# Bank choice, late evictions, a shared copy and earlier loads in a fused attention and Fourier-mixing kernel

## The chip, the cores and the metric

The kernel runs on one core of a Trainium2 chip. The metric is the device time of one execution in microseconds (us), the median of several runs. In the profile, PE is the matmul engine (PEld its weight loads), DVE the vector engine, ACT the scalar engine, POOL the GpSimd engine; SP only issues DMAs. L658 means line 658 of the kernel before.

## What is computed

Sequence length S = 2048, width D = 512, H = 32 heads of 16. All data are float32.

```python
g = sigmoid((x * gate_w).sum(-1, keepdims=True))
q, k, v = heads(x @ wqkv)
a = merge(softmax(q @ k.T * 16**-0.5) @ v) @ wo         # attention, 32 heads
b = Cr @ (x @ Wr.T) - Ci @ (x @ Wi.T)                   # real part of a 2-D DFT, dense matrices
out = g * a + (1 - g) * b
```

## The kernel before, in words

Heads go in 16 pairs, one head on each half of the PE's rows (j = 0 and 1, partitions 0 to 63 and 64 to 127). Two matmuls on different halves run beside each other, so the PE's work comes in slots of two.

Softmax needs the maximum of each query's scores before the exponentials, so each pair's scores are computed twice. A **scan** is a score matmul of 128 queries by 512 keys whose bank of PSUM is reduced to maxima by DVE (`scan`, L699 and L701). A **score** is the matmul for the exponentials (`score`, L668), read by ACT (L658), which writes a tile e in SBUF; there are 17 of these. Each step of 128 keys by 1024 queries has four scores (two of each half), and its **values** are four fp32 matmuls of e into one bank, `pvb` (`pv`, L678), each recorded as two. There are 512 steps, 32 for each pair; after every 16 the sums in `pvb` are copied to SBUF (`quotients`, L710) and later divided (`divide`). **Products** (`fill`, L919) are the matmuls of the large DFT, split in high and low parts, in banks z0 and z1. 48 products for each half make a group of 128 rows, and its two sums are evicted by DVE (`close` in `spectral`, L828 and L830) in the place where the last product is issued.

The program has four stages:

- **Front**: projections and the small DFT (`products`, L340 and L356), with the first 368 scans woven in, one pair of scans in 2.05 slots (`beside`, L186; ACT does a first pass, L190, and DVE a second, L192). `load_scan_beside` loads the keys and queries of the next head pair, 16 DMAs on ACT's queue, one every four slots, from the 37th scan of the first pair and the 21st of the others on. Their buffers are a ring of 12 (`piece`), in which the large weight loads (`load_w`, L408, on SP's queue) take turns too.
- **Single steps**: 42 rounds m of two steps, without products: `e0 e1 c0 c1 e0 e1` and then the values of one step. `values(2 * m + i)` gives the values of the step before the one just scored.
- **Fill rounds**: rounds 42 to 233, of two steps each: 8 scores, 6 scans and 16 products, then the values of two steps.
- **Mix rounds and end**: rounds 234 to 255, scores with the products of the output projection, and the last sums.

The order within a round is written out by hand. In a fill round it is

```python
"c0 e1 c0 e1 s0 s1 s0 s1 s0 s1 e0 s1 c0 e1 s1 s0 c1 e0 s1 s0 s1 s0 s0 c1 e1 s0 e0 s1 e0 c1"
```

where c is a scan, e a score, s a product, and the digit the half. We call the scans in their order S1 to S6 and the scores E1 to E8: the round runs S1 E1 S2 E2 E3 S3 E4 S4 E5 S5 E6 E7 E8 S6, with products between them. A group of products ends with the last `s0` and the last `s1` of a round, every sixth round, ahead of S6.

Scores and scans of a fill round share five banks, b0 to b4. Which bank one takes is settled by a planner, `Banks`, that keeps a clock of its own while the program is written: a bank is reckoned free 635 ns after the start of its exponential or 735 ns after that of its reduce. Of the five banks it takes the one with the least `max(s, free)`, plus 30 ns where the bank last served the other kind; among equals, the one longest free. In the single steps seven banks are in use: b0 to b3 for scores and b4, z0, z1 for scans.

Of the kernel before, what the change touches and what calls it, by code (L numbers as in the profile page):

```python
# [32 lines left out]
SCANS = 64  # L33
TOTAL = SCANS * NP
FRONT = 5 * SCANS + 48
# [6 lines left out]
SINGLES = 42  # L42
# [17 lines left out]
def build(tc, x, xT, wqkv, wo, wrT, wiT, cr, ci, gate, out):  # L60
    nc = tc.nc
    with ExitStack() as ctx:
# [55 lines left out]
        class Rows:  # L118

            def __init__(self):  # L120
                self.q, self.k = [None, None], [None, None]
# [129 lines left out]
        with ExitStack() as px:  # L251
# [11 lines left out]
            def after(n, f, *args):  # L263

                count[0] += 1
                due.append((slots[0] + n, count[0], f, args))

            def run_due(force=False):
                while True:
                    ready = [d for d in due if force or d[0] <= slots[0]]  # L270
                    if not ready:
                        return
                    d = min(ready, key=lambda d: d[:2])
                    due.remove(d)
                    d[2](*d[3])

            def load_scan_beside(p):
                rows, loads = scanned.setdefault(p, Rows()), []
                for part in PARTS:
                    load_part(rows, None, p, part, nc.scalar if p else nc.sync, kf_d, True, loads.append)  # L280
                for n, load in enumerate(loads):
                    after((4 if p else 2) * n, load)

            def scan_at(spacing):
                pace[0] = spacing
# [1 line left out]
            def beside():  # L287

                slots[0] += 1
                run_due()  # L290
                if pace[0] is None:
                    return
                pace[1] += 1.0 / pace[0]
                while seen[0] < FRONT and pace[1] >= 1.0:
                    pace[1] -= 1.0
                    n = seen[0]
                    if n % SCANS == (36 if n < SCANS else 20) and n - n % SCANS + SCANS < FRONT:
                        load_scan_beside(n // SCANS + 1)
                    if n == FRONT - SCANS + 8:
                        used[0] = Rows()  # L300
                        for part in PARTS:
                            load_part(used[0], "use", 0, part, nc.sync, k_d, True)
                    if n == FRONT - SCANS + 30:
                        first_rows.append(Rows())
                        for part in PARTS:
                            if part != "q0" or FRONT % SCANS < SCANS // 2:
                                load_part(first_rows[0], "scan", FRONT // SCANS, part, nc.sync, k_d, True)
                    scan_folded(n, 0, scan_bank)
                    done = behind(n - 1)
                    seen[0] += 1  # L310
                    if seen[0] == FRONT:
                        done = behind(n)
                    if done is not None and done % SCANS == SCANS - 1:
                        for d, part in enumerate(shift(done // SCANS)):
                            after(3 + 4 * d, part)

            def behind(n):
                if n in FOLDED:
                    scan_folded(n, 1, scan_bank)
                    return n  # L320

            behind_, ends = [], {}
# [61 lines left out]
            if True:  # L384
# [197 lines left out]
                while behind_:  # L582
                    follow()
                    beside()
# [5 lines left out]
        with ExitStack() as pa:  # L590
# [4 lines left out]
            def bank(tag, name="s"):  # L595
                return psl.tile([P, 512], F32, tag=tag, name=name)
# [3 lines left out]
            pvb = bank("pv", "pvb")  # L600
# [11 lines left out]
            class Banks:  # L612

                slot, late, gap, load, group, weights, second = 226.0, 425.0, 93.0, 207.0, 854.0, 103.0, 56.0
                switch = 30.0
                period, release = {"e": 475.0, "c": 682.0}, {"e": 635.0, "c": 735.0}
                names = [f"b{i}" for i in range(5)] + ["z0", "z1"]

                def __init__(self):
                    self.t, self.port, self.rows, self.swap = 0.0, 0.0, [0.0, 0.0], [0.0, 0.0]  # L620
                    self.free, self.last, self.count = [0.0] * 7, list("eeeeccc"), 7
                    self.engine, self.values = {"e": 0.0, "c": 0.0}, False

                def take(self, kind, j):
                    if self.values:
                        t = self.t = self.port = self.t + self.load - self.weights
                        self.rows, self.swap, self.values = [t, t], [t, t + self.second], False
                    s = max(self.port, self.swap[j])
                    if kind != "s":
                        group = (range(4) if kind == "e" else range(4, 7)) if self.count == 7 else range(5)  # L630
                        b = min(group, key=lambda b: (
                            max(s, self.free[b]) + self.switch * (self.last[b] != kind), self.free[b]))
                        self.last[b] = kind
                        s = max(s, self.free[b])
                    self.port = s + self.weights
                    self.t = self.swap[j] = max(self.port, self.rows[j], self.t + 6.0)
                    self.rows[j] = self.t + self.slot
                    if kind == "s":
                        return None
                    a = max(self.engine[kind], self.t + self.late)  # L640
                    self.engine[kind], self.free[b] = a + self.period[kind], a + self.release[kind]
                    return self.names[b]
# [64 lines left out]

            def quotients(p, h):
                ob = ap.tile([P, 512], F32, tag="ob", name="ob", bufs=2)
                nc.vector.tensor_copy(ob, pvb)  # L710
                lc = sm.tile([P, 16], F32, tag="lc", name="lc")
                for n, (c, j, r) in enumerate(quads):
                    nc.gpsimd.dma_start(lc[32 * n:32 * n + 32, :],  # L713
                                        ob[r + DH:r + VC, :].rearrange("p (s e) -> p s e", e=16))
                return p, h, ob, lc
# [200 lines left out]
            def emit(pr_, j, ps):  # L916
                group = pr_.group
                group.count[j] += 1
                nc.tensor.matmul(ps, pr_.lhs(j), pr_.rhs(j), start=group.count[j] == 1,  # L919
                                 stop=group.count[j] == group.size)  # L920
                if group.count[j] == group.size:
                    group.close(j, ps)

            def fill(j):

                if at[j] == len(stream):
                    stream.extend(next(source))
                pr_ = stream[at[j]]
                at[j] += 1
                banks.take("s", j)  # L930
                if pr_.enter and pr_.done == 0:
                    pr_.enter()
                if j not in pr_.group.banks:
                    pr_.group.banks[j] = bank(f"z{j}", "z")
                emit(pr_, j, pr_.group.banks[j])
                pr_.done += 1
                if pr_.leave and pr_.done == 2:
                    pr_.leave()

            freed = []  # L940
            staged, now = {}, [0]
            operands = output_operands()

# [76 lines left out]
            def values(n):  # L1020
                while valued[0] < n:
                    pv(valued[0])
                    valued[0] += 1

            for m in range(MACROS):
# [12 lines left out]
                p, half = divmod(m, NB)  # L1038
# [18 lines left out]
                n = min(scans)  # L1057
# [3 lines left out]
                if m < SINGLES:  # L1061
                    for i in range(2):
                        for k, token in enumerate(ORDERS[(count_ + 1 - i) // 2].split()):
                            {"e": score, "c": scan}[token[0]](int(token[1]))
                            if late and k == 3:
                                late.pop(0)()
                        values(2 * m + i)
                    continue
                for k, token in enumerate(ORDERS[count_, sizes[m]].split()):
                    {"e": score, "c": scan, "s": fill}[token[0]](int(token[1]))  # L1070
                    if late and k in (6, 13, 20):
                        late.pop(0)()
                values(2 * m)
            assert min(scans) == TOTAL, scans
            for step in (STEPS - 2, STEPS - 1):
# [15 lines left out]
            ob = ap.tile([P, 512], F32, tag="ob", name="ob", bufs=2)  # L1091
# [19 lines left out]
            c, ps = halves_[0], spread[0]  # L1111
# [8 lines left out]
            c, ps = halves_[1], spread[1]  # L1120
# [39 lines left out]
```

## Time and profile before

| | |
|---|---|
| runs before | 1748.30, 1748.83, 1749.85 us; median 1748.83 |
| profiled execution, its own time | 1747.27 us |
| its span in the profile | 1745.50 us |
| PE, ACT, DVE, POOL busy | 99%, 77%, 72%, 39% of the span |
| front | to about 351.7 us |
| single steps | to about 525 us |
| fill rounds | to about 1614 us |
| mix rounds and end | to 1745.5 us |

Times in rows are microseconds from the span's start. In a row of the timeline the first number is the start, the second the time to the end of the last of its instructions (x5 means five in a row); a bracket gives the idle time of that engine just before, and what ended it. A matmul's row that begins together with its weight load is about 0.11 us longer than the others: the load's time is in it.

### The profile page before, as it was taken

How to read it: one execution, taken by the hardware profiler on the slowest of the kernel's cores; microseconds unless marked ns; L12 is line 12 of the kernel's file. 1: busy time of each engine (PE TensorE's matmuls, PEld its weight loads, DVE VectorE, ACT ScalarE, POOL GpSimd, SP SyncE). 2: the span in 40 equal slices, each digit the busy share in tenths (PEclk: the TensorE clock that was granted, in tenths of full speed). 3: DMA queues.
4: the chain of work that ended last, by engine and by line, in shares of the span. 5: the costliest groups of instructions: out<-in, count | busy, mean ns of one | idle time of the engine just before them, and what ended most of it. 6: DMA issues, size and time to landing. Idle time of an engine off the chain costs nothing.

```text
span 1745.5 us, 36709 instructions
## 1 busy us (share of the span) xinstructions
PE 1721.8 (99%) x13657; PEld 1037.1 (59%) x13657; DVE 1264.3 (72%) x2385; ACT 1351.7 (77%) x2589; POOL 688.2 (39%) x860
## 2 busy tenths in 40 slices
PE   8999999999999999999999999999999999999998
PEld 7776788743445555555555555556555555555554
DVE  5598899866667777777777777777777777777433
ACT  5588988799997777777777777777777777777785
POOL 0263301353654443444444434434443443443121
PEclk9999999999999999999999999999999999999999
DMA  7575233564442333232333257323332422425522
GB/s 260 203 233 153 80 122 124 174 199 124 137 128 83 94 96 96 63 109 62 87 88 94 67 155 218 106 83 102 96 87 81 126 76 79 114 85 147 150 57 100
DMA packets 140003, 206.59 MB, mean 118 GB/s; under 512 B 58848, under 2 KB 61392, under 8 KB 139824
## 3 DMA queue, kind: packets, MB, share of 16 engines
q1 hardware_dynamic: 94992, 167.46, 31.4%
q0 software_dynamic: 41056, 27.86, 6.1%
q10 hardware_dynamic: 3776, 8.92, 1.8%
q8 instruction: 107, 1.75, 0.4%
q14 instruction: 72, 0.59, 0.1%
HBM read 137.89 MB, written 65.81 MB: 117 GB/s over the span
## 4 chain that ended last, share of the span: by engine, by line
PE 93%; DVE 1%; DMA 1%; issue 1%; ACT 1%; POOL 0%; SPq 0%; DVEq 0%; ACTq 0%
PE pvb L678 27%; PE z L919 23%; PE s L699 14%; PE s L668 14%; PE xy L340 6%; PE s L186 5%; PE xy L356 4%; DMA wraw<-wrT 0%; ACT fold L190 0%; DVE y L864 0%; DMA lc<-ob 0%; DVE fold L192 0%; DMA q_d<-el 0%; SPq L156 0%; DVE mx L701 0%
## 5 line engine op out<-in xcount | busy, mean ns | idle before, releaser
L658 ACT ACTIVATE e<-s 128x512 f32<-128x512 f32 x2048 | 1075.8, 600 | 298.9 <-PE s L668 251.2
L701 DVE TENSOR_REDUCE mx<-s 128x1 f32<-128x512 f32 x1312 | 860.3, 686 | 294.6 <-PE s L668 200.1
L668 PE MATMUL s<-qs,ks 50*128 50x512 f32 x2048 | 640.6, 425 | 0.0
L699 PE MATMUL s<-ks,qs 48*128 48x512 f32 x1312 | 500.9, 427 | 1.0 <-DVE mx L701 0.5
L678 PE MATMUL pvb<-e,va 128*17 128x512 f32 x4096 | 497.2, 595 | 0.0
L919 PE MATMUL z<-b,chi 64*128 64x512 f32 x2060 | 485.7, 392 | 0.0
L668 PEld LDWEIGHTS s<-qs,ks 50*128 50x128 f32 x2048 | 333.8, 184 | 118.3 <-ACT e L658 74.7
L699 PEld LDWEIGHTS s<-ks,qs 48*128 48x128 f32 x1312 | 215.4, 185 | 202.0 <-issue 118.2
L919 PE MATMUL z<-b,clo 64*128 64x512 f32 x1030 | 307.8, 392 | 0.0
L919 PEld LDWEIGHTS z<-b,chi 64*128 64x128 f32 x2060 | 280.7, 186 | 32.0 <-issue 0.8
L192 DVE CUSTOM_DVE_ANT_0 fold<-s,fold 128x512 f32<-128x512 f32 x368 | 242.8, 689 | 32.1 <-ACT fold L190 13.9
L186 PE MATMUL s<-ks,qs 48*128 48x512 f32 x736 | 237.4, 403 | 6.3 <-ACT fold L190 5.9
L244 POOL CAST chi<-craw 128x512 fp32r<-128x512 f32 x126 | 77.4, 614 | 399.1 <-PE z L919 390.3
L190 ACT ACTIVATE fold<-s 128x512 f32<-128x512 f32 x368 | 204.3, 604 | 34.2 <-PE s L186 28.3
L678 PEld LDWEIGHTS pvb<-e,va 128*17 128x17 f32 x4096 | 90.0, 96 | 218.9 <-issue 217.7
L919 PEld LDWEIGHTS z<-b,clo 64*128 64x128 f32 x1030 | 157.1, 186 | 17.0
L245 POOL TENSOR_TENSOR clo<-craw,chi 128x512 fp32r<-128x512 f32 x126 | 161.8, 1284 | 10.5
L186 PEld LDWEIGHTS s<-ks,qs 48*128 48x128 f32 x736 | 135.4, 185 | 45.0 <-ACT fold L190 17.8
L713 POOL DMA_DIRECT2D lc<-ob x124 | 63.2, 515 | 228.1 <-DVE ob L710 227.2
L356 PE MATMUL xy<-w,b 64*128 64x512 f32 x384 | 122.4, 403 | 0.0
L340 PE MATMUL xy<-w,b 64*128 64x512 f32 x384 | 118.1, 395 | 0.0
L864 DVE SCALAR_TENSOR_TENSOR y<-z,g,y 128x512 f32<-128x512 f32 x44 | 32.5, 749 | 65.3 <-PE z L919 63.6
(128 smaller groups left out, 1505.1 us busy)
## 6 DMA issues: line engine op xcount, KB each, us to landing
craw<-cr SPq DMA_DIRECT2D x64, 256.0 KB
craw<-ci SPq DMA_DIRECT2D x64, 256.0 KB
qs<-q_d SPq DMA_DIRECT2D x110, 128.0 KB
ks<-k_d SPq DMA_DIRECT2D x108, 128.0 KB
ab_d<-ab SPq DMA_DIRECT2D x32, 256.0 KB
y_d<-y SPq DMA_DIRECT2D x32, 256.0 KB
b<-bs_d SPq DMA_DIRECT2D x32, 256.0 KB
o_d<-oh POOLq DMA_DIRECT2D x28, 256.0 KB, 9.5
```

What stands on the lines that cost most here:

```text
L186: nc.tensor.matmul(ps, rows.q[qb // 8][b:b + 48, qb % 8 * P:(qb % 8 + 1) * P], rows.k[c // 2][b:b + 48, c % 2 * 512:(c % 2 + 1) * 512], st ...
L190: seen_by(nc.scalar.activation(fold[j], ps, AF.Relu))
L192: seen_by(nc.vector.tensor_tensor_reduce(out=fold[j], in0=ps, in1=fold[j], scale=1.0, scalar=-3.0e38, op0=ALU.add, op1=ALU.max, accum_out= ...
L245: sub(lo, raw, hi.bitcast(F32))
L340: ins = nc.tensor.matmul(ps, lhs[64:P], rhs[64:P], start=False, stop=last)
L356: nc.tensor.matmul(ps, lhs[0:64], rhs[0:64], start=n == 0, stop=False)
L658: nc.scalar.activation(e, ps, AF.Exp, scale=SCALE)
L668: nc.tensor.matmul(ps, rows.k[kb // 8][b:b + 50, kb % 8 * P:(kb % 8 + 1) * P], rows.q[h][b:b + 50, c * 512:c * 512 + 512], start=True, sto ...
L678: nc.tensor.matmul(pvb[r:r + VC, :], va[:, kb, 2 * p + j, :], es[step][c, j][0], start=kb == 0, stop=kb == NB - 1, tile_position=(0, r))
L699: nc.tensor.matmul(ps, rows.q[qb // 8][b:b + 48, qb % 8 * P:(qb % 8 + 1) * P], rows.k[c // 2][b:b + 48, c % 2 * 512:(c % 2 + 1) * 512], st ...
L701: nc.vector.tensor_reduce(mx[p][:, j, qb, c:c + 1], ps, axis=AX.X, op=ALU.max)
L919: nc.tensor.matmul(ps, pr_.lhs(j), pr_.rhs(j), start=group.count[j] == 1, stop=group.count[j] == group.size)
```

## The change

Six edits:

1. The DMAs of `load_scan_beside` for pairs after the first are three slots apart, not four.
2. They start with the 29th scan of the first pair, not the 37th, and with the 9th of the others, not the 21st.
3. `Banks` takes the bank with the earliest `free`, and the 30 ns for a change of kind are gone. In the single steps scores have five banks (b0 to b3 and z0), scans two (b4 and z1).
4. From round 42 on, `pvb` is copied by ACT (columns 0 to 255) and DVE (256 to 511), not by DVE alone.
5. The evictions of a group that ends in a round are issued behind all scans and scores of the round, ahead of its values.
6. In single steps the values are two steps behind the scores, not one.

```diff
-                    after((4 if p else 2) * n, load)
+                    after((3 if p else 2) * n, load)
...
-                    if n % SCANS == (36 if n < SCANS else 20) and n - n % SCANS + SCANS < FRONT:
+                    if n % SCANS == (28 if n < SCANS else 8) and n - n % SCANS + SCANS < FRONT:
                         load_scan_beside(n // SCANS + 1)
...
-                switch = 30.0
...
-                    self.free, self.last, self.count = [0.0] * 7, list("eeeeccc"), 7
+                    self.free, self.count = [0.0] * 7, 7
...
-                        group = (range(4) if kind == "e" else range(4, 7)) if self.count == 7 else range(5)
-                        b = min(group, key=lambda b: (
-                            max(s, self.free[b]) + self.switch * (self.last[b] != kind), self.free[b]))
-                        self.last[b] = kind
+                        group = ((0, 1, 2, 3, 5) if kind == "e" else (4, 6)) if self.count == 7 else range(5)
+                        b = min(group, key=lambda b: self.free[b])
...
-                nc.vector.tensor_copy(ob, pvb)
+                if now[0] < SINGLES:
+                    nc.vector.tensor_copy(ob, pvb)
+                else:
+                    nc.scalar.copy(ob[:, 0:256], pvb[:, 0:256])
+                    nc.vector.tensor_copy(ob[:, 256:512], pvb[:, 256:512])
...
                 if group.count[j] == group.size:
-                    group.close(j, ps)
+                    closing.append((group, j, ps))
...
-                        values(2 * m + i)
+                        values(2 * m + i - 1)
                     continue
...
+                for group, j, ps in closing:
+                    group.close(j, ps)
+                closing.clear()
                 values(2 * m)
```

More of the change, by code (lines that the diff above doesn't have):

```diff
@@ L932, in fill @@
                     pr_.enter()
+                assert not closing or pr_.group is closing[0][0], "a group ends within a round"
                 if j not in pr_.group.banks:
@@ L938, in fill @@
                     pr_.leave()
-            freed = []
+            freed, closing = [], []
             staged, now = {}, [0]
```

## The prediction

> **What bounds the kernel now.** I read the busy time by stage first, then the chain of work that ended last, then the timeline of single rounds. The profiled execution took 1747.27 us, its span is 1745.50.
>
> ```profile
> span 1745.5 us, 36709 instructions
> 0.00:351.70 351.70, 337.77 (x2696) 265.72 (x2696) 279.61 (x832) 273.37 (x536) 103.39 (x101) 0.99 0.52 168
> 351.70:525.00 173.30, 173.14 (x1193) 69.72 (x1193) 116.36 (x190) 172.84 (x342) 92.88 (x132) 1.00 0.51 149
> 525.00:1614.00 1089.00, 1088.49 (x8780) 634.96 (x8780) 816.82 (x1287) 810.78 (x1529) 465.56 (x592) 1.00 0.35 99
> 1614.00:1745.50 131.50, 122.44 (x997) 66.69 (x996) 51.52 (x79) 94.70 (x185) 26.40 (x37) 0.99 0.36 103
> ```
>
> The columns behind the length are the busy times of PE, PEld, DVE, ACT and POOL, then clock, DMA share and GB/s. PE seems full everywhere, but its ends are modelled, so its busy share can't show a short wait. In the single steps (second row) ACT is full too, and the timeline of ACT shows it without any gap:
>
> ```profile
> 351.70 173.28 ACT L658 ACTIVATE e<-s 128x512 f32<-128x512 f32 x341
> ```
>
> 341 exponentials in 173.28 us are 0.508 us each. **The single steps are ACT's**, and no order of banks or values there can bring anything. In the fill rounds ACT and DVE are busy three quarters of the time, and the chain of waits lies on PE. It gives the rounds' lengths, by the starts of the values' matmuls:
>
> ```profile
> 530.40 1.84 PE pvb L678 x16
> 536.05 1.84 PE pvb L678 x16
> 541.71 1.84 PE pvb L678 x16
> 547.36 1.84 PE pvb L678 x16
> 553.02 1.84 PE pvb L678 x16
> 558.86 1.84 PE pvb L678 x16
> 564.65 1.84 PE pvb L678 x16
> ...
> 1609.18 1.89 PE pvb L678 x16
> ```
>
> A plain round takes 5.65 us (541.71 to 547.36). The one from 553.02 takes 5.84: a group of products ended just before it. The one from 558.86 takes 5.79: `pvb` is copied in it. From the first to the last row lie 189 rounds in 1078.78 us, 10.9 more than 189 times 5.65. Counted from the code, 31 of them follow the end of a group and 23 hold a copy: 31 x 0.19 + 23 x 0.14 = 9.1 of the 10.9.
>
> **Plain rounds (edit 3).** Where a plain round loses time shows in its timeline (weight loads first, then reduces and exponentials):
>
> ```profile
> 546.16 0.39 PE L919 MATMUL z<-b,clo 64*128 64x512 f32 x1
> 546.17 0.18 PEld L699 LDWEIGHTS s<-ks,qs 48*128 48x128 f32 x1
> 546.82 0.18 PEld L668 LDWEIGHTS s<-qs,ks 50*128 50x128 f32 x1
> 546.82 0.18 PEld L699 LDWEIGHTS s<-ks,qs 48*128 48x128 f32 x1
> 546.98 0.39 PE L699 MATMUL s<-ks,qs 48*128 48x512 f32 x1
> 544.02 3.38 DVE L701 TENSOR_REDUCE mx<-s 128x1 f32<-128x512 f32 x5 [1.58 <-PE s L668]
> 544.05 2.72 ACT L658 ACTIVATE e<-s 128x512 f32<-128x512 f32 x5 [1.20 <-PE s L668]
> ```
>
> The weights of S5 are loaded at 546.17, when its slot has begun (546.16), not ahead of it. Worked through with the planner's rule, S5 takes the bank of S3. S3's reduce is third in DVE's run, so it ends about 544.02 + 3 x 0.68 = 546.06. Half 1 is thus 0.11 late to the end, where S6 starts at 546.98. The bank of E3 is free earlier: its exponential is third in ACT's run and ends near 545.7. The old rule leaves it to E6, because both banks count as free by the planner's clock and the 30 ns speak for the same kind. The new rule takes the one with the earlier time: S5 gets E3's bank, E6 that of S3, and E6 comes a slot (0.23) later, when the reduce is done. So the wait goes. Worked on, the other banks of the round stay as they are, but for S2 and E2 at its start, which change places and have banks free for a microsecond.
>
> What is late next is E8: it needs E5's bank, whose exponential ends at 544.05 + 2.72 = 546.77, and its load at 546.82 follows. E8 and S6 can then both start at 546.93, instead of S6 at 546.98. So a plain round gains **0.05 us**, not 0.11. Bounds: 0 (the pair of loads still ends the same way) to 0.11. For the 135 rounds that follow no group's end and hold no copy: 135 x 0.05 = 6.8 us gained.
>
> **Rounds behind a group's end (edit 5).**
>
> ```profile
> 552.96 0.74 DVE L828 TENSOR_SCALAR y<-z,gm 128x512 f32<-128x512 f32 x1
> 553.82 0.75 DVE L830 SCALAR_TENSOR_TENSOR y<-z,gm,y 128x512 f32<-128x512 f32 x1
> 554.49 0.68 DVE L701 TENSOR_REDUCE mx<-s 128x1 f32<-128x512 f32 x1
> 554.78 0.18 PEld L699 LDWEIGHTS s<-ks,qs 48*128 48x128 f32 x1 [0.85 <-DVE y L830]
> 555.22 0.18 PEld L699 LDWEIGHTS s<-ks,qs 48*128 48x128 f32 x1 [0.25 <-DVE mx L701]
> ```
>
> The two evictions stand ahead of S6's reduce, which ends at 555.17, and S2, which has S6's bank, waits 0.25. The 0.85 a row above, put down to the eviction, is the usual wait behind the values' matmuls and no loss. With the evictions behind the scan, its reduce ends 1.5 us earlier (0.74 + 0.75) and this wait goes. What is late next: the evictions, which ended at 554.57, 1.6 us after the values' first matmul, now end behind a reduce (0.68) that itself waits some 0.2 for its matmul: at about 2.5. The round's first loads come at 1.8 (554.78), the second pair's 0.11 later, and those of the first products, which want z0 and z1, a slot (0.23) behind that, near 2.2. The first eviction is done by then, the second not: half 1 starts its products some 0.24 late, and half 0, queued behind that load, about 0.1. As half 1 has 0.07 to spare before S6, I reckon 5.75 us for this round: **0.11 less** than before, with bounds of 0 and 0.24 (as a new plain round). 31 x 0.11 = 3.4 us gained. The store of the sums on SP's queue waits for the second eviction, and the queue's loads behind it come up to 1 us later; they are loaded rounds ahead.
>
> **Rounds with a copy (edit 4).**
>
> ```profile
> 560.83 0.69 DVE L710 COPY ob<-pvb 128x512 f32<-128x512 f32 x1 [1.25 <-PE pvb L678]
> 561.44 1.28 DVE L701 TENSOR_REDUCE mx<-s 128x1 f32<-128x512 f32 x2
> 562.17 0.18 PEld L699 LDWEIGHTS s<-ks,qs 48*128 48x128 f32 x1 [0.31 <-DVE mx L701]
> ```
>
> The copy delays S1's reduce to 561.44, and S3, which has its bank, waits 0.31. If the halves were copied side by side, DVE would be held for the 0.42 below only. But in the front ACT and DVE read one bank in turn, and the second waits for the first:
>
> ```profile
> 27.57 0.69 DVE L446 TENSOR_TENSOR el<-xy,eh 128x512 fp32r<-128x512 f32 x1 [0.52 <-ACT eh L445]
> 28.29 0.59 ACT L448 COPY s<-xy 128x512 f32<-128x512 f32 x1 [0.76 <-DVE el L446]
> L371 DVE TENSOR_TENSOR w<-raws,w 128x256 fp32r<-128x256 f32 x8 | 3.2, 418 | 0.0
> L370 ACT CAST w<-raws 128x256 fp32r<-128x256 f32 x8 | 3.0, 404 | 0.0
> ```
>
> ACT's copy only reads the bank `xy` and writes a tile of its own, and yet it starts when DVE's reading of the bank ends (28.26). The Trainium skill, page "PSUM — Partial Sum Buffer", section "PSUM bank collisions raise a hardware error", gives the reason: two engines may not use the same bank in the same 32 partitions at once, not even to read different columns of it, so software must keep them apart. By that rule the trace agrees with its 0.76 us of waiting, and the edit cannot run side by side.
>
> So DVE's half stands behind ACT's. With the 256-column rows as nearest prices: 0.40 for ACT, 0.03 to hand over, 0.42 for DVE, 0.85 where the whole copy took 0.69. S1's reduce starts 0.16 later than before. S3 waits for it, and behind S3 everything does. So such a round costs **0.16 more**: 23 x 0.16 = 3.7 us lost. Bounds: side by side it would gain 0.19 (to a new plain round), 4.4 in all; with PSUM halves no shorter than whole ones (0.59 and 0.69) it would cost 0.6, 14 in all. I stay with the rows of 256 columns. ACT's part lies in its 1.20 us of idle time before E1.
>
> **Single steps (edits 3 and 6).** Nothing as long as ACT stays fed; it now has five banks ahead of it. Two banks for scans suffice: a step's two reduces must end within the step's 4 x 0.508 = 2.03 us and take 2 x 0.68. But the values of one step move from the last round that ACT bounds into round 42, which PE bounds: 1.84 / 2 = 0.92, less one exponential of lead (0.51). **0.4 us lost**, with bounds of 0 and 0.9.
>
> **The front (edits 1 and 2).**
>
> ```profile
> 140.56 8.25 DMA wraw<-wrT
> 148.84 0.31 ACTq L156
> 126.10 0.58 ACTq L156 DMA_DIRECT2D ks<-kf_d  x1
> 178.05 0.58 ACTq L156 DMA_DIRECT2D ks<-kf_d  x1
> 226.33 0.58 ACTq L156 DMA_DIRECT2D ks<-kf_d  x1
> 273.35 0.58 ACTq L156 DMA_DIRECT2D ks<-kf_d  x1
> ```
>
> The chain goes from the weight load `wrT` to a DMA of ACT's queue: the third pair's loads meet that transfer, ACT stands behind its own DMA issue, and the folds behind that. The first DMAs of the pairs, 64 scans apart, show the price: 51.95 us for the stretch with the meeting, 48.28 and 47.02 for the next two, so 3.7 to 4.9. The edit starts these loads 12 scans earlier, 12/64 of 47 = 8.8 us, and closes them up by a quarter, so that the last is issued some 14 us earlier: 126.10 + 21.5 - 14, near 134 (64 scans are 131 slots, so a slot is 0.36 us, and 60 slots 21.5). The meeting goes. In exchange the second and fifth pairs' loads now straddle the other two weight loads, and ACT issues DMAs at a denser pace. Of the 3.7 to 4.9 I count **3 us gained**; bounds: 5 gained, 4 lost (one other meeting of that price).
>
> **Sum.** -6.8 - 3.4 + 3.7 + 0.4 - 3.0 = -9.1 from 1747.27 is 1738.2. The median of the runs shown lies 1.56 above the profiled execution, so I predict **1739.8 us**.
>
> **Rivals.**
>
> - *The bank swap brings nothing* (0.22): something else holds S6, most likely E8's bank alone, and plain rounds stay at 5.65. For it: E8's and S6's loads start together already (546.82). Against: S6 starts 0.05 after E8 could. 1739.8 + 6.8 = 1746.6.
> - *The copies run side by side* (0.12): 23 x (0.16 + 0.19) = 8 less, 1731.8. Against it stand the rows from 27.57. The skill's rule is what excludes it, the rest of the sum would be the same.
> - *Slower: ACT's queue can't take the denser loads* (0.08). If each of the five groups of loads on it meets a wait as the third pair's did (4.3 us, the middle of 3.7 and 4.9), the front has five of them where it had one, and is 17.2 longer than now instead of 3 shorter: 1739.8 + 20.2 = 1760.0. It decides where the queue frees up more slowly than one DMA in three slots (1.08 us). Against: the last stretch, at four slots (1.43 us), shows no such wait.
>
> **How the numbers follow.** The forecast has 0.48, the rivals 0.42, and 0.10 is left for what I don't see. From no change a measurement of this kernel can tell about 0.2%, 3.5 us: faster means under 1745.3. Faster are the forecast but for 0.02, the second rival, 0.08 of the first (where the front brings its 5) and 0.05 of the rest: 0.71. Within 0.2% are the other 0.14 of the first, the 0.02 and 0.01 of the rest: 0.17. Slower are the third and 0.04 of the rest: 0.12. The forecast's own range is 1734 to 1745. The range 1731 to 1749 takes in the side-by-side copy and the useless swap, and leaves out the slow front and a little below.
>
> **What would show it.** Plain rounds of 5.60 with S5's weights loaded a slot ahead, and E8 and S6 starting together; rounds behind a group's end near 5.75 with S6's reduce ahead of the evictions; copy rounds near 5.95 with DVE's half starting where ACT's ends; the ACT row of the single steps as long as now; no wait for `wrT` in the chain. I am wrong where plain rounds come out at 5.65 or more, or where the front has a new wait on ACT's queue.

## The result, and where the time went

| | before | after |
|---|---|---|
| median of 4 runs, us | 1748.57 | 1734.18 |
| lowest and highest | 1748.15, 1749.85 | 1732.68, 1735.69 |
| profiled execution, its own time | 1747.27 | 1734.79 |
| its span | 1745.5 | 1732.8 |

The ratio is 0.9917, with the interval [0.9899, 0.9934]: 14.4 us less, where 9.0 were forecast. The busy times of the single steps after the change, from the table of windows, columns as before:

```profile
351.70:525.00 173.30, 171.99 (x1209) 71.75 (x1205) 117.03 (x192) 169.89 (x345) 91.99 (x131) 0.99 0.51 147
```

In the single steps ACT does three exponentials more than before in the same stretch, in 3 us less of busy time: it looked full before and no longer does. The chain gives the rounds, by the starts of their values:

```profile
529.35 1.84 PE pvb L675 x16
...
540.57 1.84 PE pvb L675 x16
546.18 1.84 PE pvb L675 x16
551.79 1.84 PE pvb L675 x16
557.38 1.85 PE pvb L675 x16
563.31 1.84 PE pvb L675 x16
...
1596.62 1.39 PE pvb L675 x9
```

A plain round takes 5.61 (5.65 before), the one behind a group's end 5.59 (from 551.79; 5.84 before), the one with a copy 5.93 (from 557.38; 5.79 before). Sorted over all 189 rounds, and with the other stages beside them, by the same starts:

| part | before, us | after, us | change | forecast |
|---|---|---|---|---|
| front, to the first exponential | 351.70 | 352.86 | +1.2 | -3.0 |
| single steps, from there to the values of round 43 | 178.70 | 176.49 | -2.2 | +0.4 |
| 135 rounds without group's end or copy | 763.5 | 756.7 | -6.8 | -6.8 |
| 31 rounds behind a group's end, mean | 5.86 | 5.62 | -7.3 | -3.4 |
| 23 rounds with a copy, mean | 5.81 | 5.93 | +2.6 | +3.7 |
| end, from the values of round 232 | 136.3 | 136.2 | -0.1 | 0 |

The lines sum to -12.6 us; the span lost 12.7. The medians lie 1.9 us further apart than the profiled executions, and 1.7 more than the spans.

**Plain rounds.** In the timeline of the weight loads of one (S5's, then E8's and S6's), S5's now lie a slot ahead, and the other two come together, as the prediction had it:

```profile
544.79 0.18 PEld L696 LDWEIGHTS s<-ks,qs 48*128 48x128 f32 x1
545.68 0.18 PEld L665 LDWEIGHTS s<-qs,ks 50*128 50x128 f32 x1 [0.22 <-ACT e L655]
545.68 0.18 PEld L696 LDWEIGHTS s<-ks,qs 48*128 48x128 f32 x1
```

The last two rows start 0.89 behind S5's; before, it was 0.65, since S5's came late. The bracket of E8's load names what is left: an exponential, as reckoned.

**Behind a group's end**, DVE's timeline:

```profile
550.50 2.04 DVE L698 TENSOR_REDUCE mx<-s 128x1 f32<-128x512 f32 x3
553.24 0.75 DVE L831 SCALAR_TENSOR_TENSOR y<-z,gm,y 128x512 f32<-128x512 f32 x1
```

S6's reduce is the last of the first row, ahead of both evictions; the second is the second row. The second eviction ends at 553.99, 2.20 us after the values' start (551.79). I had reckoned with 2.5, and with the products of half 1 waiting for it.

**Copy rounds**, timeline of ACT, DVE and the weight loads:

```profile
559.35 0.37 ACT L710 COPY ob<-pvb 128x256 f32<-128x256 f32 x1 [0.86 <-issue]
559.75 0.42 DVE L711 COPY ob<-pvb 128x256 f32<-128x256 f32 x1 [1.61 <-ACT ob L710]
560.09 1.28 DVE L698 TENSOR_REDUCE mx<-s 128x1 f32<-128x512 f32 x2
560.83 0.18 PEld L696 LDWEIGHTS s<-ks,qs 48*128 48x128 f32 x1 [0.43 <-DVE mx L698]
```

DVE's half stands behind ACT's, 559.35 + 0.37 + 0.03 = 559.75, and S3 waits 0.43 for the reduce behind it, where it waited 0.31.

**Single steps**, ACT's timeline, which was one row without a gap before:

```profile
352.86 5.98 ACT L655 ACTIVATE e<-s 128x512 f32<-128x512 f32 x12
...
361.80 102.03 ACT L655 ACTIVATE e<-s 128x512 f32<-128x512 f32 x208 [0.63 <-PE s L665]
...
495.40 1.08 ACT L655 ACTIVATE e<-s 128x512 f32<-128x512 f32 x2 [0.69 <-PE s L665]
```

The long row has 208 exponentials in 102.03 us, 0.491 each against 0.508 before (a row's length holds the last record whole). In exchange there are gaps, at the beginning (0.63 ahead of this row) and near 495 (0.69).

**Front.** The wait for `wrT` has left the chain, and another has come in:

```profile
87.38 8.50 DMA wraw<-wqkv
95.90 0.31 ACTq L156
```

It is the same meeting 53 us earlier: a weight load of SP's queue, and ACT standing behind a DMA issue of its own. The 8.50 are the load's time from its issue to its end; ACT itself goes on in between and stands for shorter times. The longest ends 0.1 behind the DMA issue of the second row:

```profile
96.31 0.60 ACT L190 ACTIVATE fold<-s 128x512 f32<-128x512 f32 x1 [1.95 <-DMA wraw<-wqkv]
```

In the meeting with `wrT`, before the change, ACT stood three times up to a DMA issue, for 1.60, 1.47 and 1.28, together 4.35. What each meeting is worth is read from the products' rows (view of the tile `xy`, matmuls of L340; the columns after the colon are shortest, median and longest in ns, then the first and the last start). First before, then after:

```profile
L340 PE MATMUL xy<-b,c x144: 385/393/498, 87.6 to 139.3; 64*128 64x512 f32 x144
L340 PE MATMUL xy<-w,b x384: 385/393/625, 139.8 to 350.7; 64*128 64x512 f32 x192
L340 PE MATMUL xy<-c,b x192: 385/393/398, 215.1 to 283.7; 64*128 64x512 f32 x192
```

```profile
L340 PE MATMUL xy<-b,c x144: 385/393/628, 88.1 to 144.3; 64*128 64x512 f32 x144
L340 PE MATMUL xy<-w,b x380: 385/393/625, 144.8 to 351.0; 64*128 64x512 f32 x190
L340 PE MATMUL xy<-c,b x192: 385/393/417, 215.7 to 284.5; 64*128 64x512 f32 x192
```

From the first `b,c` to the first `w,b` it took 52.2 us and now takes 56.7; from there to the first `c,b` 75.3 and now 70.9. The meeting with `wrT` was worth 4.4 us and went; the one with `wqkv` is worth 4.5 and came. The price isn't fixed: in the eight kernels below that keep these loads, the first stretch took 54.5 to 57.1, which is 2.3 to 4.9 more than 52.2.

### The profile page after: what moved, and what is told of

Same layout as the page of the kernel before. It is cut to its first block, busy times and chain, and to the rows that moved or that the text cites. A ratio compares the mean times of both kernels' runs of the same rounds, so it can differ in the third digit from the quotient of the medians.

```text
span 1732.8 us, 36968 instructions
## 1 busy us (share of the span) xinstructions
PE 1708.2 (99%) x13657; PEld 1026.9 (59%) x13657; DVE 1249.2 (72%) x2385; ACT 1358.7 (78%) x2615; POOL 687.7 (40%) x860
## 4 chain that ended last, share of the span: by engine, by line
PE 88%; DMA 4%; POOL 2%; issue 2%; DVE 1%; ACT 1%; SPq 0%; ACTq 0%; DVEq 0%; POOLq 0%
PE pvb L675 25%; PE z L920 21%; PE s L696 15%; PE s L665 12%; PE xy L340 5%; PE s L186 5%; PE xy L356 4%; DMA bs_d<-ol 1%; DMA o_d<-ol 1%; DMA wraw<-wqkv 0%; POOL ol L964 0%; ACT fold L190 0%; DVE y L865 0%; POOL el L275 0%; DMA lc<-ob 0%
## 5 line engine op out<-in xcount | busy, mean ns | idle before, releaser
L698 DVE TENSOR_REDUCE mx<-s 128x1 f32<-128x512 f32 x1312 | 850.6, 687 | 284.3 <-PE s L665 194.9
L665 PE MATMUL s<-qs,ks 50*128 50x512 f32 x2048 | 656.7, 423 | 0.0
L696 PE MATMUL s<-ks,qs 48*128 48x512 f32 x1312 | 487.9, 419 | 1.8 <-DVE mx L698 1.4
L920 PE MATMUL z<-b,chi 64*128 64x512 f32 x2060 | 471.9, 392 | 0.0
L665 PEld LDWEIGHTS s<-qs,ks 50*128 50x128 f32 x2048 | 338.7, 184 | 133.9 <-ACT e L655 110.4
L920 PE MATMUL z<-b,clo 64*128 64x512 f32 x1030 | 300.9, 392 | 0.0
L186 PE MATMUL s<-ks,qs 48*128 48x512 f32 x736 | 237.8, 404 | 5.6 <-ACT fold L190 5.3
L340 PE MATMUL xy<-w,b 64*128 64x512 f32 x384 | 117.9, 395 | 0.0
```

The lines of the kernel that those rows point to most:

```text
L186: nc.tensor.matmul(ps, rows.q[qb // 8][b:b + 48, qb % 8 * P:(qb % 8 + 1) * P], rows.k[c // 2][b:b + 48, c % 2 * 512:(c % 2 + 1) * 512], st ...
L340: ins = nc.tensor.matmul(ps, lhs[64:P], rhs[64:P], start=False, stop=last)
L665: nc.tensor.matmul(ps, rows.k[kb // 8][b:b + 50, kb % 8 * P:(kb % 8 + 1) * P], rows.q[h][b:b + 50, c * 512:c * 512 + 512], start=True, sto ...
L696: nc.tensor.matmul(ps, rows.q[qb // 8][b:b + 48, qb % 8 * P:(qb % 8 + 1) * P], rows.k[c // 2][b:b + 48, c % 2 * 512:(c % 2 + 1) * 512], st ...
L698: nc.vector.tensor_reduce(mx[p][:, j, qb, c:c + 1], ps, axis=AX.X, op=ALU.max)
```

## The experiments

The theory after the result: the copy loses because two engines read the bank in turn; part of what the group's end gains comes from edit 5, part from the banks; the single steps were bound by the way of a bank from exponential back to score; the front traded one meeting for another. The rivals are named with each experiment. Diffs are against the changed kernel. Ratios are to the kernel before, with their intervals.

### The copy: one engine or two

`copy_dve` copies with DVE alone, as before:

```diff
-                if now[0] < SINGLES:
-                    nc.vector.tensor_copy(ob, pvb)
-                else:
-                    nc.scalar.copy(ob[:, 0:256], pvb[:, 0:256])
-                    nc.vector.tensor_copy(ob[:, 256:512], pvb[:, 256:512])
+                nc.vector.tensor_copy(ob, pvb)
```

> The changed kernel (1734.2 us) with the sums copied by DVE alone, as before the change. My theory: the two halves run one after the other, so sharing the copy costs. The 23 copy rounds, 5.93 us in the changed kernel, go to about 5.80, all other rounds stay: 23 x 0.13 = 3 us faster, 1731. Rival, that the shared copy relieves DVE: copy rounds get longer than 5.93, and the kernel is slower.

Measured: 1731.46 us, 0.9904 [0.989, 0.9919]; copy rounds 5.81. So the split copy costs 2.7 us in the trace, 0.12 in each of the 23 rounds; the intervals of the times overlap.

`copy_act` gives the whole of it to ACT from round 42 on:

```diff
-                    nc.scalar.copy(ob[:, 0:256], pvb[:, 0:256])
-                    nc.vector.tensor_copy(ob[:, 256:512], pvb[:, 256:512])
+                    nc.scalar.copy(ob, pvb)
```

> The changed kernel with the sums copied by ACT alone from round 42 on. My theory: what lengthens copy rounds is only that DVE's first reduce starts late; ACT has 1.2 us of idle time there, and its chain of exponentials is held by the matmul of E3 anyway, which comes 1.1 us after that of E1. A whole copy on ACT (about 0.59 us) delays E1 by some 0.1 and nothing behind it: copy rounds at 5.60 to 5.65, 23 x 0.3 = 7 us faster than the changed kernel, 1727. Rival: ACT's chain sets the round's end by E8, so a delay of E1 of 0.1 to 0.2 goes on to the end: copy rounds of 5.7 to 5.8.

Measured: 1726.89 us, 0.9876 [0.9862, 0.9889]. Its chain and its timeline:

```profile
558.00 1.85 PE pvb L675 x16
563.61 1.84 PE pvb L675 x16
```

```profile
559.96 0.59 ACT L710 COPY ob<-pvb 128x512 f32<-128x512 f32 x1 [0.89 <-issue]
```

The copy lies in ACT's idle time, the exponentials follow it within 0.5 us, DVE has no part in it, and the round takes 5.61, no more than a plain one. All 189 rounds take 1060.0 us, 7.3 less than after the change. So the cost of the split was not that the copy exists but that DVE took part in it. The two halves side by side weren't tried: both lie in one bank, and another layout of `pvb` would be another kernel. They also write one tile, `ob`; that the bank alone makes the second engine wait is read from the prediction's rows at 27.57 and 28.29, not from these.

### The group's end and the banks

`evict_in_place` undoes edit 5 alone. The rival was that the gain behind a group's end is the new bank rule's.

```diff
-                    closing.append((group, j, ps))
+                    group.close(j, ps)
```

> The changed kernel with the evictions of a group issued in place again, ahead of S6. My theory: the 31 rounds behind a group's end, 5.62 in the changed kernel, go back to about 5.84 as S6's reduce is late for the bank that the next round's second pair takes: 31 x 0.23 = 7 us slower, 1741. Rival: the new order of banks alone removes that wait (E2 takes that bank now, not S2), and the time stays at 1734.

Measured: 1740.80 us, 0.9957 [0.9942, 0.9972]. Rounds behind a group's end have a mean of 5.75, between 5.86 and 5.62. Chain and timeline of one:

```profile
552.51 1.85 PE pvb L675 x16
558.25 1.84 PE pvb L675 x16
```

```profile
553.98 0.68 DVE L698 TENSOR_REDUCE mx<-s 128x1 f32<-128x512 f32 x1
554.71 0.18 PEld L665 LDWEIGHTS s<-qs,ks 50*128 50x128 f32 x1
```

S6's reduce again ends late, at 554.66, but with the new rule its bank goes to E2 (the load at 554.71), not to S2. Both theories have a part: the bank rule alone brought 0.11 us a round, and the moved evictions another 0.12 on top of it. The 189 rounds take 1071.4 us, 4.2 more than after the change, 3.9 of them in these 31 rounds. The medians are 6.6 apart. The front in this profile is 1.4 longer and the single steps 0.7 shorter, with the same code; the rest wasn't traced. So the expected 1741 came out, but the rounds account for 4.2 of the 7 us that it was worked out from.

`fill_old_rule` puts the old rule back for the five banks of the fill rounds alone:

```diff
-                    self.free, self.count = [0.0] * 7, 7
+                    self.free, self.last, self.count = [0.0] * 7, list("eeeecec"), 7
...
-                        b = min(group, key=lambda b: self.free[b])
+                        if self.count == 7:
+                            b = min(group, key=lambda b: self.free[b])
+                        else:
+                            b = min(group, key=lambda b: (
+                                max(s, self.free[b]) + 30.0 * (self.last[b] != kind), self.free[b]))
+                        self.last[b] = kind
```

> The changed kernel with the old rule for the five banks of the fill rounds (longest free of those free now, 30 ns against a change of kind); the single steps stay as changed. My theory: S5 waits for S3's bank again, plain rounds go from 5.60 to 5.65, 130 of them: 6.5 us slower, 1741. Rival: the 0.05 came from something else (the later values, the evictions), and plain rounds stay at 5.60.

Measured: 1743.48 us, 0.9974 [0.9961, 0.9988]. Its chain:

```profile
533.51 1.84 PE pvb L680 x16
539.16 1.84 PE pvb L680 x16
...
556.11 1.84 PE pvb L680 x16
561.76 1.84 PE pvb L680 x16
...
1608.78 1.39 PE pvb L680 x9
```

Plain rounds are back at 5.65, and the 189 rounds take 1075.27 us against 1067.27: the rule of the banks is 8.0 us in the fill rounds. The round behind a group's end (from 556.11) took 5.65 as well, and the mean of all 31 is 5.66. So edit 5 doesn't need the rule: under the old rule it brings 0.20 (5.86 to 5.66), under the new one 0.12. What each is worth behind a group's end depends on whether the other is there; the two gains don't simply add. The other 1.3 us of the 9.3 between the medians may lie in the single steps, which took 179.0 us in this profile with the changed kernel's code for them (176.5 there): DVE waits 4.07 us for a DMA ahead of the inversion at 496.06. That this comes with the edit wasn't shown.

### The front

`second_pair_late` keeps edits 1 and 2 but for the second pair, whose loads start and are spaced as before:

```diff
-                    after((3 if p else 2) * n, load)
+                    after((4 if p == 1 else 3 if p else 2) * n, load)
...
-                    if n % SCANS == (28 if n < SCANS else 8) and n - n % SCANS + SCANS < FRONT:
+                    if n % SCANS == (36 if n < SCANS else 8) and n - n % SCANS + SCANS < FRONT:
```

> The changed kernel, but the second pair's loads begin with the 37th scan and are four slots apart, as before the change; the other pairs' loads stay as changed. My theory: the change freed the third pair's loads of the meeting with one weight load and brought the second pair's into the same with another (4 us each), so that the front won nothing. With the second pair's loads behind that weight load again, both meetings are gone: 4 us faster than the changed kernel, 1730. Rival: the wait belongs to the front and moves on to other loads: 1734.

Measured: 1730.62 us, 0.9902 [0.9888, 0.9916]. No weight load is left in its chain, and the products' rows have both gains:

```profile
L340 PE MATMUL xy<-w,b x384: 385/393/628, 140.4 to 348.4; 64*128 64x512 f32 x192
L340 PE MATMUL xy<-c,b x192: 385/393/399, 211.4 to 280.7; 64*128 64x512 f32 x192
L340 PE MATMUL xy<-b,c x144: 385/393/488, 88.3 to 140.0; 64*128 64x512 f32 x144
```

52.1 us for the first stretch (56.7 after the change) and 71.0 for the second (70.9). So each pair meets its own weight load, and the two prices are independent.

`front_undone` undoes edits 1 and 2. The rival was that they gain something outside of the two meetings.

```diff
-                    after((3 if p else 2) * n, load)
+                    after((4 if p else 2) * n, load)
...
-                    if n % SCANS == (28 if n < SCANS else 8) and n - n % SCANS + SCANS < FRONT:
+                    if n % SCANS == (36 if n < SCANS else 20) and n - n % SCANS + SCANS < FRONT:
```

> The changed kernel with both edits of the front undone: loads four slots apart, from the 37th scan of the first pair and the 21st of the others on. My theory: the meeting with a weight load goes back from the second pair's loads to the third's, at the same price, so the time stays at that of the changed kernel, 1734 with 1.5 either way. Rival: earlier loads are worth something beyond the meetings: 1736 or more.

Measured: 1734.11 us, 0.9925 [0.9912, 0.9938]. That can't be told from the changed kernel's 0.9917. The chain has the old meeting again:

```profile
140.38 8.34 DMA wraw<-wrT
```

So edits 1 and 2 as they stand bring nothing that a measurement shows.

### The single steps

Three kernels undo the two edits singly and together; a fourth moves what I took for the price of edit 6. The rival to the banks as bound was my prediction's: ACT's own pace.

`values_one_late` undoes edit 6:

```diff
-                        values(2 * m + i - 1)
+                        values(2 * m + i)
```

> The changed kernel with the values one step behind the scores in the single steps, as before the change; five banks for scores and two for scans stay. In the changed kernel an exponential of the single steps takes 0.492 us where it took 0.508. Theory A, the fifth bank for scores did it: the stretch of single steps stays, and one step's values fall out of round 42 again (0.9 us): 1733. Theory B, the later values did it: the single steps go back to 2.03 us each, 84 x 0.06 less 0.9: 1738.

`single_banks_4_3` undoes the five and two banks:

```diff
-                        group = ((0, 1, 2, 3, 5) if kind == "e" else (4, 6)) if self.count == 7 else range(5)
+                        group = ((0, 1, 2, 3) if kind == "e" else (4, 5, 6)) if self.count == 7 else range(5)
```

> The changed kernel with four banks for scores and three for scans in the single steps, as before the change; the values stay two steps behind. Theory A (the fifth bank did it): the single steps go back to 2.03 us each, 84 x 0.06 is 5 us slower, less some 2.5 us of waits for the two scan banks that go: 1736 to 1739. Theory B (the later values did it): the single steps stay at 1.97, and the waits for the scan banks go: 1732.

`single_steps_undone` has both of these edits:

```diff
-                        group = ((0, 1, 2, 3, 5) if kind == "e" else (4, 6)) if self.count == 7 else range(5)
+                        group = ((0, 1, 2, 3) if kind == "e" else (4, 5, 6)) if self.count == 7 else range(5)
...
-                        values(2 * m + i - 1)
+                        values(2 * m + i)
```

> The changed kernel with both edits of the single steps undone: values one step behind, four banks for scores and three for scans, though still taken by the earliest time. Both theories: single steps of 2.03 us as before the change and the values of one step out of round 42; the stretch from the first exponential to the values of round 43 is 178.6 us as before the change, 2.2 more than in the changed kernel: 1736.4. If it stays at 1734, the rule for taking banks made the single steps faster.

| kernel | banks | values late | median, us | ratio | single steps, us |
|---|---|---|---|---|---|
| the change | 5/2 | 2 steps | 1734.18 | 0.9917 [0.9899, 0.9934] | 176.5 |
| `values_one_late` | 5/2 | 1 step | 1731.64 | 0.99 [0.9885, 0.9915] | 172.5 |
| `single_banks_4_3` | 4/3 | 2 steps | 1738.80 | 0.9953 [0.9938, 0.9968] | 182.1 |
| `single_steps_undone` | 4/3 | 1 step | 1737.01 | 0.9938 [0.9921, 0.9956] | 178.6 |

The last column goes from the first exponential to the values of round 43. The fifth bank brings 6.1 us with the values one step late (178.6 - 172.5) and 5.6 with two; values two steps late cost 4.0 with five banks and 3.5 with four. The medians move the same way, though some of their intervals overlap. One trace of each is thin: the six other kernels with the changed kernel's single steps took 175.2 to 179.0 for them. The longest row of ACT in `values_one_late`, `single_banks_4_3` and `single_steps_undone`:

```profile
353.26 167.22 ACT L655 ACTIVATE e<-s 128x512 f32<-128x512 f32 x341
```

```profile
360.45 166.79 ACT L655 ACTIVATE e<-s 128x512 f32<-128x512 f32 x328 [1.22 <-PE s L665]
```

```profile
353.86 174.94 ACT L655 ACTIVATE e<-s 128x512 f32<-128x512 f32 x344
```

All three are without a gap, but their paces are 0.490, 0.509 and 0.509. What tells them apart is the duration of a single record. The groups of ACT's exponentials between 365 and 460 us, of the kernel before and of the changed one (busy time, then the mean ns of one), and behind them the group of the fill rounds before, 540 to 1590 us, where ACT idles:

```profile
L658 ACT ACTIVATE e<-s 128x512 f32<-128x512 f32 x189 | 95.8, 602 | 0.2
```

```profile
L658 ACT ACTIVATE e<-s 128x512 f32<-128x512 f32 x1472 | 781.4, 597 | 269.5 <-PE s L668 224.4 <-PE s L699 29.5 <-PE z L919 8.2
```

```profile
L655 ACT ACTIVATE e<-s 128x512 f32<-128x512 f32 x196 | 96.2, 936 | 0.0
```

Before, one takes 602 ns, as long as where ACT waits for work (597). Record by record, the trace shows why: as long as ACT goes on without waiting, each record is some 0.01 us longer than the one before it, and it falls back to 0.60 where ACT has waited. Before the change that happens at the first exponential of every step. The records overlap by some 0.1 us, and so this wait leaves no gap to see. After the change the records grow to some 0.95 in this stretch and don't fall back, and 196 exponentials lie in these 95 us instead of 189.

What ACT waited for shows in single records of one step before the change:

```profile
401.43 1.09 ACT L658 ACTIVATE e<-s 128x512 f32<-128x512 f32 x2
401.91 0.50 PE L668 MATMUL s<-qs,ks 50*128 50x512 f32 x2
402.45 0.60 ACT L658 ACTIVATE e<-s 128x512 f32<-128x512 f32 x1
402.57 0.18 PEld L668 LDWEIGHTS s<-qs,ks 50*128 50x128 f32 x1
```

The step's first exponential (402.45) begins 0.04 behind the end of its matmul (401.91 + 0.50), so it waited for its score. The step's fourth score is loaded at 402.57, 0.05 behind the end of the exponential four before (401.43 + 1.09), so it waited for the bank; the values come behind it on PE, and the next step's first score behind the values. That closes the circle. Over the 95 us the fourth load comes 0.05 behind the exponential four before it in all three kernels' traces with four banks, and behind the one five before it in those with five (medians). With five the pace is 0.490 whether a step's first score is ready 0.04 (the change) or 0.10 ahead of its exponential (`values_one_late`), so it no longer hangs on when the score comes: as far as these runs show, ACT sets it there.

Where edit 6 loses shows first in the changed kernel, in a wait of DVE for a DMA and in the scan behind it:

```profile
493.40 0.25 DVE L721 RECIPROCAL lc<-lc 128x16 f32<-128x16 f32 x1 [2.52 <-DMA lc<-ob]
494.25 0.18 PEld L696 LDWEIGHTS s<-ks,qs 48*128 48x128 f32 x1 [1.31 <-DVE mx L698]
```

The sums' copy comes a step later than before, the inversion that reads them through a DMA keeps its round; DVE stands still, and its reduces with it. `invert_later` gives the inversion two rounds more:

```diff
-                    for n, f in zip((3, 6, 9) if m < SINGLES else (2, 4, 6) if p < NP - 1 else (2, 3, 4), divide(*quotients(p, h))):
+                    for n, f in zip((5, 8, 11) if m < SINGLES else (2, 4, 6) if p < NP - 1 else (2, 3, 4), divide(*quotients(p, h))):
```

> The changed kernel (values two steps behind), with the inversion of the sums and what follows it issued two rounds later in the single steps (5, 8 and 11 rounds behind the copy, not 3, 6 and 9). With the values one step behind, the stretch from the first exponential to the values of round 43 took 172.4 us; in the changed kernel it takes 176.4. Theory: with later values the copy of the sums comes a step later, but the inversion keeps its round, so DVE waits for the DMA of the sums (2.5 us in one place) with the scans queued behind it; of the 4 us some 2 to 2.5 go: 1732. Rival: the 4 us lie in the moved values and at the start of the steps alone: 1734.

Measured: 1731.64 us, 0.9909 [0.9894, 0.9924], the single steps 174.6 us. DVE no longer waits for this DMA, and ACT's timeline has no gap any more from 359.25 on, 328 exponentials in 161.06 us, 0.491 each. So 1.9 of the 4.0 us were this wait, as far as one trace of each tells; the intervals of the times overlap. The other 2.1 are gaps at the beginning and the values moved into a round that PE bounds (forecast as 0.9 less a lead). The first 16 exponentials take 8.94 us here (350.31 to 359.25), where 0.490 each would make 7.84; that leaves about 1.1 for the gaps and 1.0 for the values.

### Both kernels beaten

`best` is the changed kernel with ACT's whole copy, the second pair's loads as before and the values one step late:

```diff
-                    after((3 if p else 2) * n, load)
+                    after((4 if p == 1 else 3 if p else 2) * n, load)
...
-                    if n % SCANS == (28 if n < SCANS else 8) and n - n % SCANS + SCANS < FRONT:
+                    if n % SCANS == (36 if n < SCANS else 8) and n - n % SCANS + SCANS < FRONT:
...
-                    nc.scalar.copy(ob[:, 0:256], pvb[:, 0:256])
-                    nc.vector.tensor_copy(ob[:, 256:512], pvb[:, 256:512])
+                    nc.scalar.copy(ob, pvb)
...
-                        values(2 * m + i - 1)
+                        values(2 * m + i)
```

> The changed kernel with what the runs showed to be better: sums copied by ACT alone from round 42 on (7.3 us), second pair's loads as before the change (3.6 us), values one step behind in the single steps (2.6 to 4 us); five banks for scores, the new rule and the late evictions stay. If the three do not overlap: 1734.2 - 14 = 1720. If two of them share a cause: 1723 or more.

Measured: 1719.07 us, 0.9838 [0.9825, 0.9852], twice the change's gain. The three corrections sum to 7.3 + 4.6 + 4.0 = 15.9 by their traces, and the medians differ by 15.1. Its chain holds one more meeting, with the third of the weight loads:

```profile
217.39 8.85 DMA wraw<-wiT
```

From the first to the last of the products `c,b` of L340, beside which this load lies, it takes 70.6 us here (211.2 to 281.8) and took 68.6 before the change; in `fill_old_rule`, whose chain holds the same load, 72.1. So it may cost 2 to 3.5 us. Whether a later start would free it wasn't tried.

## Why the prediction was right where it was, and wrong elsewhere

**The time** lay in the range of 1731 to 1749, and at 1734.2 just inside the forecast's own of 1734 to 1745. Of the 12.7 us that the span lost the sum had 9.1, with two terms of the wrong sign and one half too small. That it came so near is in part luck: the front was 4.2 us worse than its term, the single steps were 2.6 better and the rounds behind a group's end 3.9.

- **Plain rounds: right, in mechanism and size** (-6.8). S5's wait went, E8's bank was next, and `fill_old_rule` brought the 5.65 back.
- **Behind a group's end: right mechanism, mis-sized** (-7.3 for -3.4). The step that failed was "at about 2.5" for the end of the second eviction. It measured 2.20: S6's reduce ended 0.75 after the values' start (550.50 + 2.04 = 552.54), not 0.9, and 1.45 later both evictions, of 0.74 and 0.75, were done. So no product waited, and the round came out at the other bound, that of a plain one. I had also put down the whole gain to edit 5. Under the old rule it does bring nearly all of it (0.20 of 0.24, `fill_old_rule`), but the banks alone would have brought 0.11 (`evict_in_place`).
- **Copy rounds: right mechanism** (+2.6 for +3.7). The trace agrees with the rule of the Trainium skill that the prediction cites (page "PSUM — Partial Sum Buffer", section "PSUM bank collisions raise a hardware error"): DVE's half waited 1.61, to the end of ACT's. That the cure was ACT alone, I could have read from its 1.20 us of idle time, into which 0.59 goes.
- **Single steps: the failed step** is "no order of banks or values there can bring anything". I took a row without gaps for a full engine, and did not look at the duration of one. The runs show a circle in its place, score, exponential, score in the same bank, whose length set the pace with four banks, 0.508 us for an exponential; with five it is ACT's, 0.490. My 0.4 for the moved values was a tenth of what they cost (4.0): it left out the reader behind them, DVE's inversion, whose round didn't move (1.9), and the gaps at the beginning (about 1.1).
- **The front: the failed step** is "of the 3.7 to 4.9 I count 3 us gained". The gain was 4.4. I named the second pair's new overlap and had one such meeting among the bounds, but in the sum I took off only about 1 us for it, though the price stood in the rows (3.7 to 4.9). It cost 4.5. That the first exponential came 1.2 later says nothing about the edits: kernels with the same front code began the single steps between 349.7 and 354.5.
- **The rivals.** The useless swap and the side-by-side copies are excluded by 5.61 and by the 1.61. ACT's queue could take the denser loads: the chain has one meeting, not five (two in five other kernels with the same loads, the second with `wiT`).

## What to carry to other kernels

An engine whose timeline has no gap isn't thereby the bound: compare the mean duration of its instruction there with that in a stretch where it idles. Here equal durations meant that it still waited once in each step, and another buffer helped. Where loads are moved away from one large transfer, look up what they now lie beside and charge the same price there. Where the producer of a value moves by a step, follow the value through every DMA to its last reader, and move that too.

## What the runs showed of the hardware

- Records of successive exponentials on ACT overlap. They followed each other every 0.508 us with a mean record of 602 ns where ACT waited once in a step, and every 0.490 where it didn't, with records of 936 (the change) or 831 (`values_one_late`). So the length of a record tells whether ACT has waited, and not its pace.
- While a weight load of SP's queue was under way, for 8.25 to 8.85 us from its issue, DMA issues on ACT's queue came late and ACT's work with them, up to 2.4 us at a time (three different loads: `wqkv` 1.95 in the change, `wrT` 1.60 before it, `wiT` 2.39 in `values_one_late`). For two of them the delay of the products was measured, 4.4 us and 2.3 to 4.9 us. What holds the issue wasn't shown: the load itself, or a store queued behind it that ACT's loads read. Moving ACT's loads to another time freed it.
- Two copies of 256 columns of one bank by two engines took 0.37 + 0.03 + 0.42 = 0.82 us in turn, longer than the whole by either: 0.59 on ACT, 0.69 on DVE.
